# A hand-kept order table replaced by another one that also carries banks, fillers and load gates

## The chip, the cores and the metric

The kernel runs on one core of a Trainium2 chip. The core has five instruction queues that run side by side and wait for each other through semaphores: TensorE (PE, matmuls into the eight banks of PSUM), VectorE (DVE), ScalarE (ACT), GpSimd (POOL, used here to issue loads) and SyncE (SP, used here to issue transposes and stores). The metric is the device time of one execution in microseconds.

## The reference

Two stages follow each other. First comes attention for 4 batches, 8 heads, 768 positions and a head size of 64, in which a query sees the 8 first keys and the 96 nearest ones, with a bias that falls with distance. Then the result, laid out as 3072 tokens by 512, goes through a feed-forward layer with a squared ReLU. All arrays are float32 in memory. Cut to what matters:

```python
scores = scale * np.matmul(q, k.transpose(0, 1, 3, 2))
is_global = pos[None, :] < 8
is_local = (rel >= 0) & (rel < 96)
dist = np.where(is_global & ~is_local, 96, np.abs(rel))
scores = np.where(is_global | is_local, scores - slopes[:, None, None] * dist, -1e9)
a = softmax(scores)
x = np.matmul(a, v).transpose(0, 2, 1, 3).reshape(3072, 512)
h = np.maximum(x @ w_in, 0.0)          # w_in 512 x 2048
out = (h * h) @ w_out                  # w_out 2048 x 512
```

## The kernel before

The 3072 tokens are worked on as eight halves of 384 tokens, two for each batch (`hb` 0 to 7, with tiles of 128 tokens). Halves 0 and 1, the opening, run tile by tile in small jobs, since the data is still coming in; the others run in larger jobs. Everything is fp16 in SBUF, and sums are kept in PSUM in float32.

The stations of a half, with the lines that the profile shows, are these. `list_loads` (L472) lists the loads of q, k and v, three tiles of 128 tokens each, issued from POOL. Weights come the same way: `w_in_sb` in four column blocks c0 to c3 (`load_w_in`, L534) and `w_out_sb` in four row blocks (L541). In the opening q and k are turned (transposed to have the head's columns on partitions) on PE, `turn_first` and its neighbours (L1318, L1361); from half 3 on they are turned by a DMA transpose on SP, `turn_by_dma` (L647), one for k (`k<-sk`) and one for q (`q<-sq`). `score_unit` (L691, in the opening L1404) multiplies q by k into `sp`; its operands use 64 of the array's 128 rows, two heads at a time. ACT takes the exponent (`ex`, L704), DVE multiplies by the mask (`phat`, L728), PE multiplies by v (`av`, `attend`, L752), and DVE divides by the sum (`tm`, L762). `to_x_by_dma` (L777) turns the result by four DMA transposes on SP, `xt<-tm`, one for each pair of heads (the X transposes below); in the opening PE does it (`trx`, L1483).

Layer 1 (`hps`, L797, and L900 for halves in which it is done with seven products of mixed blocks in place of eight) multiplies by `w_in_sb`. The mixed blocks `x_mix` (L878) are made of xt on DVE. The ReLU and the square run on ACT and DVE (`hr`, `h`, `kept`). Layer 2 (`yps`, L1052, and L1138 for pairs of halves done by seven products) multiplies by `w_out_sb` or its mixed blocks `w_mix`; ACT or DVE copies or adds the result to `y` (L336, L338, L1200), and SP, once ACT, stores it (L1068, L1212, L1219, L1223). `L336` and `L338` are the two lines of `copy` for ACT and for DVE.

The order is not left to a scheduler. Each job of a station is an `Op` in one of three lists: PE's jobs (letter p), loads (l), and the rest. A table of words, `ORDER`, names for each step an engine (p, l, a for ACT, d for DVE, g for POOL, s for SP) and an index of the list; the ops are emitted in that order, so the table fixes each engine's queue, and for ops that could run on ACT or on DVE also the engine. While it walks the table, `Plan.run` keeps a small model of the time: it picks the PSUM banks that in the model come free first (`idle_banks`), and it gives a PE job in the first 24 us that in the model must wait a number of filler matmuls on zeros ahead of it (`warm`, L404 and L353), which keep PE busy. A load's order on the POOL queue comes from the table; what it must wait for comes from the code. There, the first k load (`sk`) of a half beyond the third waits for both turns of the half before, and the k turn of a half waits for the last of its q loads, and so for all of its q and k loads.

Of the kernel before, what the change touches and what calls it, by code (L numbers as in the profile page):

```python
# [41 lines left out]
AFTER = [0, 0, 0, 0, 0, 0, 0, 0]  # L42
# [10 lines left out]
ORDER = """d1 g2 a4 p0 a6 s8 d12 a0 s10 d17 l3 d13 l1 a18 a16 a19 l2 d21 d20 a27 l5 a26 d14 a22 d15 d3 a28 d5  # L53
p10 l4 a25 d9 p5 a30 d146 l0 a24 p1 a11 p2 d7 l6 a23 p3 l10 a32 d31 a33 d34 p6 l9 a29 d36 p7 a39 p11
d35 l7 p8 a46 p4 d43 p9 a41 l8 d37 p13 d44 a40 p12 d45 a47 l11 p14 d38 p16 a42 p15 d48 l13 p17 d51
a49 p19 p24 a52 l12 d55 p20 d64 p22 a50 p23 d58 l14 a53 p34 d56 p30 a60 p25 d71 p28 l16 p21 a81 d59
p26 d57 a82 l18 p27 d69 d67 p31 a65 d68 p18 a61 p29 l15 d72 p36 p32 a54 d70 p35 l19 a86 d66 p33 a73
d85 p39 d62 p40 l17 a74 a77 d76 p37 l21 d91 a78 p41 l20 d79 d63 p38 d83 l23 a101 d75 d84 p45 l22 a89
a87 d96 p44 l27 p47 a92 d80 p48 d107 a97 l29 d111 p46 a98 p52 l28 p43 a93 d110 p53 p42 d105 l30 d119
p55 d120 p50 l24 p59 a122 a88 d90 d99 a102 p51 l25 d106 a103 d94 p49 a116 a128 d108 p67 d100 a129  # L60
d95 a117 d112 p57 a104 p65 d125 p54 p58 d121 d189 p63 p61 p62 a132 d126 a109 p60 a114 d135 d118 a113
d115 p56 a127 d205 d191 a133 p74 a130 p72 a169 d138 p73 a165 d131 p77 d123 a166 p69 a167 p75 d156
d147 a157 p70 p71 d134 a158 p82 d159 l34 a162 d168 p81 a163 d186 l26 a170 p83 a142 p68 l31 d174 a139
d160 d149 p84 l35 a184 a164 d208 p64 a187 d124 l33 d161 a171 d148 a144 p85 l32 d272 a143 d206 p88
d207 l36 p89 d201 p79 d151 p86 a198 a178 d204 p91 d152 a195 a199 d188 p76 d202 a136 d150 p87 a172
d200 a179 p90 a196 d180 a193 p80 d153 a209 p78 s194 l37 p66 d155 a175 d203 a137 p95 d210 p92 a176
d223 a173 p94 d197 s224 l38 a185 d177 p100 a211 l39 d236 a181 s216 p93 a140 d237 p96 a182 p103 d238
s217 p97 d183 a244 a240 d221 a141 p102 d219 a222 d154 p106 s220 d213 d225 p98 p104 d239 s226 p99
d227 d228 p105 a234 d214 s229 d145 a218 d243 p101 l44 d245 d246 p107 l43 s215 d212 a241 d190 p109
l40 p110 p108 p111 a255 d192 l42 a251 p112 a256 d258 l45 a248 d257 p113 l41 a249 d230 d232 a252 p118  # L70
d259 p114 a273 d253 s260 l46 p116 d254 p115 a261 p120 d231 d250 l47 a262 p122 a264 p124 l48 s235
d280 p123 a265 d263 p131 a268 d233 a283 p127 d281 p126 a288 p132 d285 a269 p134 d295 s328 a287 p129
d270 a286 p119 a291 p142 d266 a293 p140 d296 s329 d314 p130 a311 p135 d267 a299 p128 d315 a292 p137
d274 a312 p136 d300 s242 p121 a305 s282 d327 a302 p125 a306 d289 p138 s275 a284 d303 p141 a307 d301
d304 a276 p117 d294 s290 a313 d308 p133 a271 l50 p139 d330 a278 p143 d297 a309 l56 p145 d279 a316
s298 p146 d310 p147 l53 a317 p144 d405 a334 l51 d322 p148 a326 a337 d323 l52 p149 a335 d443 d340
a331 l49 p151 d324 a341 p150 a332 d336 p152 l54 a342 d318 d325 p157 a348 p153 a343 d333 a345 d344
p159 p156 a346 d320 d319 a354 d407 p158 a356 p161 d321 a338 p172 d355 a359 p154 d349 p162 d377 a351
p169 p163 d360 a372 s378 l57 p164 d363 p167 a361 p166 d365 p171 d347 a368 p177 s408 a369 p160 d339
p165 a364 p170 a362 d357 p178 s409 l55 d373 a386 p175 a366 p173 a387 d382 p180 a367 p174 d376 p182  # L80
d374 p176 a379 s247 d383 p155 d380 s277 a384 s358 p179 d391 a385 p181 d395 a375 p168 s381 d353 d410
a393 p183 l58 a352 p184 d388 a370 a397 d394 l65 s396 p185 a392 d389 a399 d371 l62 p187 a398 d390
p188 p186 a419 l59 p189 d411 a415 a423 d412 l63 p190 a420 d426 a416 p191 d422 l73 a424 d414 a417
p192 l61 d421 a428 d425 p193 p194 p196 a432 l60 d413 a427 d418 a429 p198 p195 a436 d406 a444 d401
a433 p200 d492 p199 d402 a437 d447 p207 a430 p210 d435 a457 p204 s448 d445 p215 a462 p211 d453 p202
s350 d463 s446 p197 d439 a451 p203 d403 a464 p218 d496 d404 p206 a442 d441 d505 a475 d493 p205 a465
d438 p208 s507 p219 a455 d434 p213 a476 p201 d468 s508 a454 d431 a458 p223 p222 a472 d497 p214 a484
d469 d452 p217 a449 p212 s400 d470 a474 p209 d482 a456 p220 p227 d459 a477 s483 d466 p224 a500 p216
d495 a478 s467 l64 p221 d498 a471 p241 d479 a486 p225 l70 p229 a509 d488 d494 l66 p226 a489 d473
p228 a511 d490 a539 l69 d480 p231 d481 p233 l72 p230 a513 d501 d487 a519 l67 d460 p234 a520 d499  # L90
a512 l71 s440 p248 d521 a485 s506 d503 p235 l68 a514 d502 d522 a546 d510 p247 a461 d491 p236 s523
l74 d524 p237 a545 p232 d515 p239 a525 d531 a516 p246 d504 a517 p256 d544 p245 a536 p270 a528 d561
s537 d543 p240 a529 p249 d518 a538 p267 a547 d530 p251 a580 p255 d550 p252 a526 s595 p258 d559 a562
p243 a551 p266 d527 p238 a585 d578 s450 a553 p253 a565 d591 p254 s579 d541 a535 d554 p261 a557 p257
d532 s560 a568 p268 a558 d533 p242 a582 d555 s596 d563 a552 p260 d534 p250 a581 p269 d548 p264 p244
a567 a586 d574 p263 d542 a564 p259 d572 p262 a540 a583 p265 d556 p272 a575 s573 a597 d566 p271 d600
s549 d569 p277 d598 a576 d584 a599 p273 d570 a577 p274 d571 p275 p276 a601 d613 a608 d615 s614 l75
p278 a602 s593 d589 d616 a609 p279 a619 d617 s594 a604 p283 d587 a620 s592 d603 a611 a605 p281 d618
a631 p280 p282 a624 d588 p286 d606 a628 a625 p284 d634 a629 p287 d610 p292 a636 p288 d607 a632 d627
a635 d686 p294 a621 p301 d630 a646 p291 d637 d643 p299 d657 a641 p314 d626 a622 p290 d680 p285 d640  # L100
p307 s681 a633 p305 d623 p300 a665 p295 d655 s642 p293 s612 d647 d590 p296 d668 a644 p298 a656 d648
p309 a658 p289 d649 p308 a670 d654 p297 p304 d638 a651 p311 d652 s639 a663 p312 p306 d669 p317 d687
s653 p310 d688 a690 p302 d676 p316 p320 a684 s677 a650 p303 a685 d674 p328 p319 d671 a662 d666 a697
a672 p313 d659 p315 d696 p331 a675 d682 p318 a660 d691 d667 d678 a719 p333 a661 p332 d689 p321 d692
a664 d683 p335 d695 a716 p352 d698 d705 s699 p347 d693 s645 p334 d742 a752 p322 d723 a722 d673 p337
p339 d679 p336 d706 p338 d700 d720 p324 d721 d728 p329 a725 d753 a724 p343 a710 d729 p341 a726 d701
s711 p342 a717 p340 d736 p323 d694 a737 d734 p344 a738 d702 p345 d709 p325 d703 a740 d708 d707 p351
a712 d731 p353 a730 p326 d727 d704 p346 d750 p348 d713 a741 p327 d732 a733 p349 d714 p357 d746 a715
a754 d735 p330 d743 a755 d739 p354 d751 d764 p350 d744 a756 p356 d718 a748 s757 d747 a745 d749 p355
d760 p362 a758 d761 p358 d765 s759 d763 p368 a770 d779 a768 d767 p364 d762 d766 p359 d769 d775 p360  # L110
d776 d786 a783 p365 d790 d780 d781 p366 a787 d777 p367 a771 a788 p371 d789 d772 d782 s773 p361 d778
d794 p369 s795 d774 p370 d791 p363 d792 s793 p372 a784 p373 d796 s785 s797 a798 a799"""


class Op:
    EARLY = {"ACT": 0.035, "DVE": 0.045}
    LATE = {"ACT": 0.1, "DVE": 0.07}

    def __init__(self, costs, emit, needs, rank=0, lag=0.0, move=None):
        self.emit, self.rank, self.lag, self.move = emit, rank, lag, move  # L120
        self.needs = [n for n in needs if n is not None]
        self.costs = {e: c - self.EARLY.get(e, 0.0) for e, c in costs.items()}
        self.done, self.bufs = None, []
        self.wait = 0.0
        self.takes, self.users, self.rows, self.follows = 0, [], False, []


class Buffer:

    def __init__(self, tag, count):  # L130
        self.tag, self.count, self.users, self.taken = tag, count, [], False
# [7 lines left out]
class Plan:  # L139
# [5 lines left out]
    HOP = 0.08  # L145
    ENTER = 0.19
# [4 lines left out]
    def __init__(self, warm_from, warm_until):  # L151
        self.warm_from, self.warm_until = warm_from, warm_until
        self.queues = {"PE": [], "LOAD": []}
        self.rest = []
        self.free = {e: 0.75 for e in ("ACT", "DVE", "POOL", "SP")}
# [54 lines left out]
    def ready(self, op):  # L210
        t = self.free_at(op)
        if t is None:
            return None
# [1465 lines left out]
```

## Time and profile before

| | |
|---|---|
| median of 3 runs | 201.06 us (200.97 to 201.07) |
| span of the profiled execution | 200.3 us |
| PE busy | 193.0 us, 96% |
| DVE busy | 178.9 us, 89% |
| ACT busy | 155.9 us, 78% |
| POOL busy | 66.7 us, 33% |
| DMA | 27.52 MB |

The execution that the profiler recorded has no time of its own beside its span; the median of the runs lies 0.76 us above that span. Busy shares of the engines are of the span. A busy PE can still be waiting in part, since the ends of matmuls are modelled. In groups and waits, `<-` names what ended an idle time. "L" with a number is a line of the kernel before.

### The profile page before, as it was taken

The numbers are of one execution on the slowest core, as the hardware profiler recorded it, in microseconds if no ns is written. First come the engines' busy times: TensorE is split into PE (matmuls) and PEld (weight loads), VectorE is DVE, ScalarE is ACT, GpSimd is POOL, SyncE is SP. The second block draws the span as 40 slices with busy tenths as digits, with TensorE's granted clock in tenths as the row PEclk, the third lists the DMA queues.
The fourth block names the chain that finished last, engine by engine and source line by source line (L and its number), as shares of the span: only waits on it lengthen the run. The fifth ranks groups of instructions, "written<-read, shape, count | busy, mean of one in ns | idle before, by whom it ended". The sixth has DMA issues, their size and how long they took to land.

```text
span 200.3 us, 5912 instructions
## 1 busy us (share of the span) xinstructions
PE 193.0 (96%) x2346; PEld 161.3 (81%) x2346; DVE 178.9 (89%) x457; ACT 155.9 (78%) x335; POOL 66.7 (33%) x82
## 2 busy tenths in 40 slices
PE   7798999999999899999999999999999999999994
PEld 2685899766897587779878798899888988899993
DVE  7688698899999799989999999999989979998881
ACT  5999676898946889988999798989996669457411
POOL 8996564087108602920095019400000000000000
PEclk9999999999999999999999999999999999999999
DMA  5999999999999999999999989995230330210214
GB/s 154 180 150 197 187 181 173 209 192 154 176 203 74 141 206 219 120 115 99 221 133 147 155 203 144 166 246 111 53 114 3 124 61 3 105 56 0 108 52 157
DMA packets 106987, 27.52 MB, mean 137 GB/s; under 512 B 97104, under 2 KB 104016, under 8 KB 106960
## 3 DMA queue, kind: packets, MB, share of 16 engines
q0 software_dynamic: 74944, 13.11, 93.3%
q1 hardware_dynamic: 30816, 13.45, 30.9%
q10 hardware_dynamic: 1200, 0.59, 1.1%
q8 instruction: 18, 0.29, 0.6%
q14 instruction: 9, 0.07, 0.1%
HBM read 27.26 MB, written 6.29 MB: 167 GB/s over the span
## 4 chain that ended last, share of the span: by engine, by line
PE 72%; DVE 12%; DMA 7%; POOL 3%; ACT 2%; issue 1%; DVEq 0%; POOLq 0%
PE yps L1138 28%; PE hps L797 17%; PE hps L900 17%; DMA w_in_sb<-in_moe_w_in_dram 4%; PE sp L691 3%; PE av L752 3%; DMA xt<-tm 3%; PE yps L1052 2%; DVE phat L728 2%; POOL w_mix L472 2%; DVE tm L762 2%; POOL v L472 1%; ACT ex L704 1%; DVE hr L958 1%; DVE mixed L1103 1%
## 5 line engine op out<-in xcount | busy, mean ns | idle before, releaser
L797 PE MATMUL hps<-xt,w_in_sb 128*128 128x384 f16 (+2 forms) x336 | 45.1, 280 | 0.2 <-DMA w_in_sb<-in_moe_w_in_dram 0.2
L704 ACT ACTIVATE ex<-sp 128x512 f16<-128x512 f32 x66 | 36.4, 632 | 2.6 <-PE sp L691 2.5
L1138 PEld LDWEIGHTS <-h 128*128 128x128 f16 x376 | 34.3, 98 | 5.1 <-DVE h L838 0.2
L797 PEld LDWEIGHTS <-w_in_sb 128*128 128x128 f16 x336 | 28.1, 98 | 7.9 <-DMA w_in_sb<-in_moe_w_in_dram 0.7
L336 ACT COPY y<-yps 128x256 f32<-128x256 f32 (+2 forms) x42 | 15.5, 389 | 17.5 <-PE yps L1138 17.3
L1138 PEld LDWEIGHTS <-mixed 128*128 128x128 f16 x272 | 25.1, 98 | 3.7 <-DVE mixed L1103 0.6
L958 DVE TENSOR_TENSOR hr<-hps,kept 128x384 f16<-128x384 f32 x49 | 25.6, 551 | 2.2 <-ACT h L998 1.1
L472 POOL DMA_DIRECT2D sq<-in_q_dram x19 | 17.2, 907 | 29.7 <-DMA q<-sq 21.6
L336 ACT COPY kept<-hps 128x384 f32<-128x384 f32 x45 | 21.1, 490 | 7.4 <-PE hps L900 4.9
L822 ACT ACTIVATE hr<-hps 128x384 f16<-128x384 f32 (+1 forms) x44 | 22.2, 530 | 4.9 <-PE hps L797 4.8
L472 POOL DMA_DIRECT2D sk<-in_k_dram x19 | 17.1, 901 | 25.3 <-DMA q<-sq 13.6
L900 PEld LDWEIGHTS <-in_mix 128*128 128x128 f16 x272 | 23.0, 98 | 2.3 <-DVE x_mix L878 0.6
L900 PE MATMUL hps<-x_mix,in_mix 128*128 128x192 f16 x204 | 23.4, 246 | 0.3 <-ACT ex L704 0.3
L1138 PE MATMUL yps<-w_out_sb,h 128*128 128x256 f16 (+1 forms) x184 | 22.5, 268 | 0.1
L1138 PE MATMUL yps<-w_mix,mixed 128*128 128x256 f16 (+1 forms) x184 | 22.4, 268 | 0.1
L1138 PE MATMUL yps<-w_mix,h 128*128 128x256 f16 (+1 forms) x192 | 22.4, 264 | 0.0
L472 POOL DMA_DIRECT2D v<-in_v_dram x24 | 21.5, 908 | 2.6 <-DMA w_mix<-in_q_dram 0.9
L728 DVE TENSOR_TENSOR phat<-ex,mask 128x1024 f16<-128x1024 f16 (+1 forms) x36 | 20.7, 598 | 0.0
L900 PEld LDWEIGHTS <-w_in_sb 128*128 128x128 f16 x204 | 17.4, 98 | 2.1 <-issue 0.7
L900 PE MATMUL hps<-xt,w_in_sb 128*128 128x192 f16 x136 | 16.1, 246 | 0.5 <-DMA xt<-tm 0.5
L998 ACT ACTIVATE h<-hr 128x768 f16<-128x768 f16 x19 | 15.9, 853 | 0.4 <-DVE hr L968 0.3
L836 ACT ACTIVATE h<-hr 128x512 f16<-128x512 f16 (+1 forms) x22 | 15.9, 742 | 0.1
(115 smaller groups left out, 363.4 us busy)
## 6 DMA issues: line engine op xcount, KB each, us to landing
out_dram<-y SPq DMA_DIRECT2D x23, 256.0 KB, 2.5
v<-in_v_dram POOLq DMA_DIRECT2D x24, 128.0 KB, 6.8
sq<-in_q_dram POOLq DMA_DIRECT2D x19, 128.0 KB, 6.7
sk<-in_k_dram POOLq DMA_DIRECT2D x19, 128.0 KB, 6.7
w_in_sb<-in_moe_w_in_dram POOLq DMA_DIRECT2D x4, 512.0 KB, 10.9
w_out_sb<-in_moe_w_out_dram POOLq DMA_DIRECT2D x4, 512.0 KB, 12.3
y<-in_q_dram SPq DMA_DIRECT2D x2, 256.0 KB, 4.4
y<-in_k_dram ACTq DMA_DIRECT2D x2, 256.0 KB, 5.1
```

The source lines that it names most:

```text
L336: nc.scalar.copy(out=out, in_=in_)
L472: dma = nc.gpsimd.dma_start(out=dst, in_=src[x.b, :, r0 + t * P:r0 + (t + 1) * P, :] .rearrange("h p d -> p h d"))
L691: nc.tensor.matmul(sp[h][:, i, :], lhsT=lhsT, rhs=x.q[rows, r % HT, a, :], start=True, stop=True)
L704: nc.scalar.activation(out=st["ex"][:, h], in_=sp[h], func=AF.Exp, scale=scale)
L728: eng(e).tensor_tensor(out=x.phat[a][:, :, t0:t0 + n], op=ALU.mult, in0=st["ex"][:, :, i0:i0 + 2 * n].rearrange("p e (t b) c -> p e t (b c ...
L797: nc.tensor.matmul(st["ps"][:, i * n:(i + 1) * n], lhsT=w_in_sb[:, kk, m * P:(m + 1) * P], rhs=x.xt[:, kk, c0:c1], start=kk == 0, stop=kk ...
L822: nc.scalar.activation(out=o, in_=i, func=AF.Relu)
L836: nc.scalar.activation(out=h2, in_=hr, func=AF.Square)
L900: nc.tensor.matmul(st[name][:, i * HC:(i + 1) * HC], lhsT=left(i, kk), rhs=right(kk), start=fresh and i == kk == 0, stop=kk == KK - 1, ski ...
L958: eng(e).tensor_tensor(out=hidden(which)[:, :, cols], in0=sums(name), in1=st[kept], op=ALU.add)
L998: nc.scalar.activation(out=h2, in_=hr, func=AF.Square)
L1138: nc.tensor.matmul(st[bank_name][:, 0:n], lhsT=a(m), rhs=b(m)[:, cols], start=fresh and m == 0, stop=m == HK - 1, skip_group_check=not fresh)
```

## The change

The operations stay the same; what stands where changes, in four ways.

1. `ORDER` is another table, with another order on each of the queues and for some ops another engine. Its words carry more. `p100.5` gives the PSUM bank of a job (`.57` two banks, 5 and 7), `+149` the filler time ahead of it in hundredths of a microsecond, and `l43@220` a gate: the load is issued only once the SP transfer 220 of the list has landed.
2. The model of the time in `Plan` (`ready`, `free_at`, `take`, `idle_banks`, `by_rank`) goes. `run` reads the table.
3. The waits of transfers in the code change. From half 4 on, a k load waits for the k turn of the half before and a q load for the q turn, where the first k load waited for both. A k turn waits for k's loads and a q turn for q's, where the k turn waited for all.
4. PE's turns of the opening also stand behind the memset of v's last column (`x.bt.op`, L485 in its `start`).

The instruction lists as built: PE 2366 matmuls for 2346, which are fillers (26 transposes of 128 columns, all ahead of the first tile's turn, for six wide matmuls); DVE 476 instructions for 459 and ACT 323 for 340; POOL and SP as many as before. The runs of 64-row score matmuls between other work are 23 for 17.

```diff
@@ (the table; one stretch of each, around 55 us, and the end)
-... d202 a136 d150 p87 a172
-d200 a179 p90 a196 d180 a193 p80 d153 a209 p78 s194 l37 p66 d155 a175 d203 a137 p95 d210 p92 a176
-...
-p370 d791 p363 d792 s793 p372 a784 p373 d796 s785 s797 a798 a799"""
+... p104 s220 d221 p106 d213 a222 d228 a218 p99 d227 s229 d154 p107 d239 a234 d212 p110.04
+s226 l43@220 p109.37 d245 p101 a255 d246 a251 l41 p111 a256 d241 s215 a252 l42@224 p116.06 s235
+d258 p114.32 s242 d257 p108.47 l40@229 p112 a248 d230 d253 d192 p120 a249 a261 d254 p118.4 a262
+p115.73 l44@226 d273 p113 a264 d231 d263 l45 p122.2 a265 d250 p124 a268 p125.7 l46 d267 a269 d280
+...
+p372 d790 p373 d796 p371 s797 a798 a799 p363 d794 s795 a784 s785"""
@@ class Plan
     def run(self):
-        order = []
-        self.in_rows = False
-        for e, op in self.by_table() if ORDER else self.by_rank():
-            start = max(self.ready(op), self.free.get(e, 0.0))
...
-            taken = self.idle_banks(op.takes) if op.takes else []
...
-            if taken and start < self.warm_until:
-                self.spare = start - 0.1 - max(idle, taken[-1][0])
-                self.spare *= 0.5 if start < self.warm_from + 5.0 else 1.0
...
+        lists = {"p": self.queues["PE"], "l": self.queues["LOAD"]}
         for word in ORDER.split():
+            word, _, spare = word.partition("+")
+            word, _, banks = word.partition(".")
+            word, _, gate = word.partition("@")
+            op = lists.get(word[0], self.rest)[int(word[1:])]
+            self.now, self.spare = [int(i) for i in banks], int(spare or 0) / 100
+            op.result = op.emit("POOL" if word[0] == "l" else self.LETTERS[word[0]])
+            if gate:
+                self.behind(op.result, self.rest[int(gate)].result)
@@ list_loads
-        before = (prev.turned if prev else []) + (halves[x.hb - 1].turned if x.hb > 2 else [])
+        if x.hb > 3:
+            before = {"sk": halves[x.hb - 1].turned[:1], "sq": halves[x.hb - 1].turned[1:]}
+        else:
+            last = halves[x.hb - 1].turned if x.hb > 2 else prev.turned if prev else []
+            before = {"sk": last, "sq": last}
...
-                if x.hb > 3 and name == "sk" and t == 0:
-                    for turn in halves[x.hb - 1].turns + (prev.xturns if AFTER[x.hb] else []):
-                        behind(dma, turn)
-                if name == "sq":
-                    x.last_load = dma
+                return dma
@@ turn_by_dma
-                if not x.turns:
-                    behind(turn, x.last_load)
                 x.turns.append(turn)
+                return turn
-            op = plan.add({"SP": 2.0 if i else 1.5}, emit, [*x.k_in, *x.q_in, x.bt.op, *late],
+            op = plan.add({"SP": 2.0 if i else 1.5}, emit, [*loads, x.bt.op, *late],
                           move=plan.TURN)
```

More of the change, by code (lines that the diff above doesn't have):

```diff
@@ L130, in __init__ @@
     def __init__(self, tag, count):
[L131 removed]
+        self.tag, self.count, self.users = tag, count, []
     def used_by(self, *ops):
@@ L189, in load @@
         return op
-    def free_at(self, op):
-        t = self.last_move if op.move else 0.0
-        for buf in op.bufs:
-            ring = self.rings.setdefault(buf.tag, [])
-            if buf.taken or ring:
-                t = max(t, buf.start if buf.taken else ring[-1].start)
-            if not buf.taken and len(ring) >= buf.count:
-                for u in ring[-buf.count].users:
-                    if u.done is None:
-                        return None
-                    t = max(t, u.done + self.HOP)
-        return t
@@ L247, in by_table, with run @@
[L247 removed]
+    def run(self):
         lists = {"p": self.queues["PE"], "l": self.queues["LOAD"]}
         for word in ORDER.split():
[L250 to L281 removed]
@@ L1642 @@
     with tc.manual_schedule():
-        order = plan.run()
+        plan.run()
 _INS = ['q', 'k', 'v', 'n_global', 'n_local', 'moe_w_in', 'moe_w_out']
```

212 lines of the change are left out of this document (73 added, 139 removed).

## The prediction

> **What bounds the kernel now.** I read the page's busy times and slices first, then the waits of TensorE (PE), its windows, the chain that ended last, and last the queues around its two weak stretches.
>
> ```profile
> span 200.3 us, 5912 instructions
> ...
> PE 193.0 (96%) x2346; PEld 161.3 (81%) x2346; DVE 178.9 (89%) x457; ACT 155.9 (78%) x335; POOL 66.7 (33%) x82
> ...
> PE   7798999999999899999999999999999999999994
> ...
> PEclk9999999999999999999999999999999999999999
> ```
>
> TensorE is busy 96% of the span at full clock; DVE stands second with 89%. So the time is PE's own work plus the few microseconds in which PE has nothing to do. The profiled span of 200.3 us lies 0.76 us under the median run of 201.06; I carry that 0.76 to the forecast.
>
> ```profile
> 20.00:30.00 10.00, 9.95 (x138) 8.98 (x139) 8.32 (x29) 6.80 (x15) 6.12 (x8) 1.00 1.76 184
> 30.00:60.00 30.00, 30.00 (x349) 24.02 (x348) 27.14 (x63) 23.54 (x53) 11.73 (x14) 1.00 1.80 184
> 60.00:70.00 10.00, 9.42 (x103) 6.30 (x102) 8.69 (x22) 7.07 (x15) 7.92 (x9) 1.00 1.70 108
> 70.00:80.00 10.00, 10.00 (x127) 8.19 (x125) 9.63 (x27) 9.26 (x22) 1.30 (x2) 1.00 1.82 211
> 80.00:90.00 10.00, 9.53 (x115) 7.47 (x112) 9.18 (x23) 9.20 (x20) 6.58 (x8) 1.00 2.29 119
> 90.00:100.00 10.00, 10.00 (x132) 8.83 (x130) 9.86 (x27) 9.05 (x19) 0.00 (x0) 1.00 1.33 156
> 100.00:110.00 10.00, 9.97 (x143) 8.36 (x141) 9.71 (x23) 9.98 (x24) 7.88 (x9) 1.00 1.97 145
> 140.00:185.00 45.00, 45.00 (x509) 40.04 (x507) 41.50 (x101) 32.80 (x69) 0.00 (x0) 1.00 0.20 59
> ```
>
> These windows list PE, weight loads, DVE, ACT and POOL. After 20 us PE idles 0.58 us in 60 to 70 and 0.47 us in 80 to 90, and next to nothing elsewhere. Before 20 us it waits for data, which ends with the first columns of w_in:
>
> ```profile
> 11.57 8.42 DMA w_in_sb<-in_moe_w_in_dram
> 20.04 3.69 PE hps L797 x40
> ...
> 45.31 0.78 PE sp L691 x24
> 46.09 0.97 PE yps L1052 x4
> 47.06 0.87 PE yps L1138 x8
> ...
> 48.58 0.86 PE yps L1052 x4
> ...
> 50.32 0.55 PE sp L691 x16
> ...
> 61.78 5.83 DMA xt<-tm
> ...
> 81.85 1.06 PE yps L1138 x8
> ...
> 83.85 1.05 PE yps L1138 x8
> ```
>
> In the chain (start, duration, work) the weights issued at 11.57 let layer 1 start at 20.0. Two later groups of eight `yps L1138` matmuls take 1.06 and 1.05 us where a full-speed one takes 0.87: 0.37 us more of PE's waiting that the windows count as busy. With 0.58 and 0.47 this makes 1.42 us lost between 60 and 90. The chain there goes back to one transfer, the DMA transpose that turns attention's result into layer 1's input (`xt<-tm`, L777), 5.83 us long.
>
> ```profile
> 58.06 4.92 SPq L777 DMA_TRANSPOSE xt<-tm  x3
> ```
>
> ```profile
> 60.67 1.75 POOL L472 DMA_DIRECT2D sq<-in_q_dram  x2 [9.90 <-DMA q<-sq]
> 62.41 1.82 POOL L472 DMA_DIRECT2D sk<-in_k_dram  x2
> ```
>
> ```profile
> 67.70 0.63 DVE L878 TENSOR_TENSOR x_mix<-xt 128x384 f16<-128x384 f16 x2 [1.17 <-DMA xt<-tm]
> ```
>
> ```profile
> PE hps L900 <- DMA xt<-tm: 0.5, 1, 0.5
> ```
>
> ```profile
> DMA to landing us min/median/max: 2.3/3.8/7.5
> ```
>
> SP issues three of these transposes from 58.06 on; POOL starts the next half's loads at 60.67, the moment the q turn has landed, beside them. DVE then waits 1.17 us for the last transpose and PE 0.5. Over all 24 transposes the time to landing runs from 2.3 to 7.5 us, so 5.83 is a crowded one.
>
> **The change part by part.** It keeps every matmul of the result and moves three things: the order on each queue, the waits of the loads and turns, and the engine of some copies.
>
> *Start.* After adds 26 idle-time transposes of 128 columns before the first tile and drops six wide fillers; the cover is the wait for the first tile. POOL's list now starts tokens without a wait: before, it lost 0.31 us to DVE's memset of v (L485), which after puts first on DVE.
>
> ```profile
> 5.41 1.84 POOL L472 DMA_DIRECT2D v<-in_v_dram  x2 [0.31 <-DVE v L485]
> ...
> 11.57 1.55 POOL L534 DMA_DIRECT2D w_in_sb<-in_moe_w_in_dram  x2
> ```
>
> The w_in load stands at the same place of POOL's list, so it issues 0.31 earlier, and layer 1 may start as much earlier: bounds 0 (if the DMA engines and not the issue set its landing) and 0.31. I take 0.30, because POOL issues back to back from there. If PE's opening work became the cover that fails, the term goes to 0.
>
> *Score runs.* Attention's scores use 64 rows of the array; each run of such matmuls costs entry and exit. From the chain: 24 matmuls take 0.78 and 16 take 0.55, so one is 0.029 and entry is 0.55 - 16 x 0.029 = 0.09; the four `yps L1052` behind a run take 0.97 against 0.86 elsewhere, so exit is 0.11. A run costs 0.20. The built order has 23 runs where before has 17. Four more stand in the opening, where PE waits for data anyway; one group of eight scores is moved behind the first layer-1 job, which costs 8 x 0.029 + 0.20 = 0.43, and two more runs stand later: 0.40. Sum +0.83, bounds 0.56 (only exit counted) and 0.95 (0.24 a run).
>
> The Trainium skill, page "TensorEngine Tiling (Array Packing)", section Key Properties, speaks against this part too: a change of tiling mode drains the array. Its page "TensorE: Matmul & The Clock Gate", section Step-by-step, gives a drain of about 128 cycles, an estimate of 0.05 us for each change at 2.4 GHz, 0.11 for a run in place of the 0.20 measured here; by it this term would be 0.56 and the forecast 200.3.
>
> *Transposes and loads.* A load word in the new table may carry a gate: it is issued only when a named SP transfer has landed. Half 4's q and k loads are gated behind half 2's X transposes (those of 58 us), and some loads of the later halves behind one transpose or another. In return k's turn waits for k's loads alone, not for the last load of all. The X transposes of 58 us thus run with no loads beside them. In the quiet case they take 2.3 instead of 5.83, 3.5 us, which is more than the 1.42 us lost, so I take all of 1.42; bounds 0 (the loads only move, and something else crowds them) and 1.42. Behind a gated load the whole POOL list waits, v's loads too; k and q of half 4 then land some 1 to 2 us later. Their turn is late only if that eats its lead. In before SP issues half 4's turns at 71.93 and 73.55:
>
> ```profile
> 71.93 1.45 SPq L647 DMA_TRANSPOSE k<-sk  x1
> 73.55 2.95 SPq L647 DMA_TRANSPOSE q<-sq  x1
> ```
>
> ```profile
> DMA to landing us min/median/max: 3.7/4.3/6.2
> ```
>
> This second row of landings is that of the turns (L647): the one issued at 73.55 lands near 78. Counted back from PE's end, the scores that need it stand at about 80 us in the new order, a lead of some 2 us for the 1 to 2 us of delay. The quiet transposes also open the gates sooner; so I take nothing, with a bound of +1.7.
>
> *Engines.* The built order gives DVE 476 instructions for 459 and ACT 323 for 340: 17 copies and squares go from ACT to DVE. Costs from these groups:
>
> ```profile
> L336 ACT COPY y<-yps 128x256 f32<-128x256 f32 (+2 forms) x42 | 15.5, 389 | 17.5 <-PE yps L1138 17.3
> ```
>
> ```profile
> L1200 DVE TENSOR_TENSOR y<-yps,y 128x256 f32<-128x256 f32 x28 | 11.7, 422 | 1.6 <-ACT ex L704 0.7 <-PE yps L1138 0.4 <-issue 0.2
> ```
>
> An op of that kind is 0.39 on ACT and 0.42 on DVE, 17 x 0.40 = 6.8 us more for DVE, from 178.9 to about 185.7, 93% of the span. Beside PE's 96% this is still cover, so it costs nothing in the sum. If the cover is gone, see the second rival.
>
> *End.* Before ends with a half-width copy and small store; after ends with an older job whose 256 columns go out whole.
>
> ```profile
> 196.50 0.37 ACT L336 COPY y<-yps 128x256 f32<-128x256 f32 x1 [3.54 <-PE yps L1138]
> ...
> 197.39 0.27 ACT L336 COPY y<-yps 128x128 f32<-128x128 f32 x1 [0.52 <-PE yps L1138]
> 197.69 0.36 ACTq L1219 DMA_DIRECT2D out_dram<-y  x1
> ```
>
> ```profile
> out_dram<-y SPq DMA_DIRECT2D x5, 256.0 KB, 2.0
> ...
> out_dram<-y ACTq DMA_DIRECT2D x1, 64.0 KB, 1.7
> ```
>
> The copy takes 0.37 for 0.27 and the store lands in 2.0 for 1.7: +0.40, with bounds 0.3 and 0.6.
>
> *Sum.* 200.3 - 0.30 + 0.83 - 1.42 + 0.40 = 199.81 us of span, plus 0.76: 200.57, called 200.6, 0.23% under 201.06. A measurement of this kernel can tell about 0.2%, that is 0.40 us, from no change: under 200.66 is faster, over 201.46 slower. The forecast lies just on the fast side.
>
> **The rivals.**
>
> *Half of it comes (no change).* The X transposes are quicker but DVE's own queue holds their users: in the rows above DVE is busy 9.63 of 10 us in 70 to 80, so an x_mix op that is released 1 us earlier may find its place in the list no earlier. Then of 1.42 half stays: 200.57 + 0.71 = 201.3. With nothing gained at all, the same sum gives 202.0. For it: DVE waited for the transposes only 1.17 us in this row, and later losses at 82 and 84 us stand behind DVE and ACT work. Against it: those losses begin with that wait.
>
> *DVE becomes the bound (slower).* DVE's idle time in 70 to 110 is 0.37 + 0.82 + 0.14 + 0.29 = 1.62 us. A proportional share of the 6.8 us moved to it, 40 of 200 us, is 1.4 us. Then DVE has no slack there; each wait that it still has for PE or ACT goes through to PE, whose banks it empties. If the 1.62 us of waits stay, PE loses up to that: 200.57 + 1.6 = 202.2. It decides from the point where more than about 0.9 us of them goes through (200.57 + 0.9 is past 201.46). For it: 9.86 busy of 10 in 90 to 100. Against it: ACT gives work away and was 9.98 busy of 10 in 100 to 110, so some of DVE's waits for ACT go, and in 140 to 185 DVE has 3.5 us to spare.
>
> *The gates hold the loads too long (slower).* A transpose with the longest landing, 7.5 for the 3.8 of the median, holds the gate 3.7 us longer; with a lead of 2 us, 1.7 us reaches the scores: 200.57 + 1.7 = 202.3. For it: everything on POOL stands behind one gate. Against it: a gated transpose is a quiet one, nearer 2.3.
>
> **How the numbers follow.** The forecast case, in which all 1.42 us or nearly all of it comes, has 0.41. No change has 0.26: half of the gain, or all of it eaten by a run price of 0.24. DVE as the bound has 0.19, late gates 0.14. So faster 0.41, same 0.26, slower 0.33. The point stays that of the likeliest, 200.6, whose own range is 199.8 to 200.66. The low end is 200.57 with the run price by exit alone (0.56 for 0.83, so 200.3), the tail at its lower bound (-0.1) and the remaining idle time of 20 to 30 and 100 to 110 (0.08) gone, and 0.3 more for waits hidden in busy time as at 82 us: 199.8. The high end, 202.3, is that of the late gates, and takes in DVE as the bound.
>
> **What would show it.** Right: PE idle under 0.2 us in 60 to 90, no row in which x_mix or hps waits for xt; first hps of layer 1 at about 19.7; transposes to landing with a maximum near 4; the last store of 256 KB on SP. The run price is right if `yps` or `hps` groups behind score runs stay near 0.1 us longer. DVE as bound would show as PE waiting for DVE (x_mix, kept, hr) and DVE over 9.8 of 10 in 70 to 110. Late gates would show as POOL waiting for `xt<-tm` and PE's `sp L691` waiting for the k or q turn. The prediction is wrong in its first step if layer 1 starts no earlier, and as a whole if PE's idle time in 60 to 110 is not smaller than before.

## The result, and the profile after

The changed kernel takes 209.3 us (median of four runs, 207.8 to 211.9) against 201.06 before: 1.036 times the time of before, with an interval of 1.028 to 1.045. The forecast was 200.6, with a range of 199.8 to 202.3. Times of one and the same kernel spread by some per cent between executions, the kernel before included (199.9 to 206.0 over all its comparison runs), so ratios with their intervals are used below, and single profiles to see where time goes. An execution more than 1.5% longer than the shortest of its kernel is left out of the ratios, and the profiles of three kernels ("v loads ungated, no fillers", "old order, new waits" and "before, memset first") are of such long executions, so what they alone show is not taken for a cause.

One base number of the forecast falls at once. Each comparison run lists its time beside its span, and the two lie 1.7 to 1.9 us apart (208.78 and 207.0 for the profile below). The 0.76 that the prediction carried compared the span of one execution with the median of others; the profiled execution of before took about 202.1 (an estimate from that distance). In spans the comparison is 200.3 before, 199.8 forecast, 207.0 after: 7.2 us off.

The page of the changed kernel, span, busy times and slices:

```profile
span 207.0 us, 5957 instructions
...
PE 197.3 (95%) x2366; PEld 164.5 (79%) x2366; DVE 183.5 (89%) x474; ACT 149.6 (72%) x318; POOL 66.9 (32%) x82
...
PE   7999999999999999499999999998999999999993
...
PEclk9999999999999999759999999999999999999999
```

One slice of PE stands out, and right behind it the granted clock falls. The waits of PE, and windows around that place (PE, weight loads, DVE, ACT, POOL, then the clock):

```profile
PE yps L1057 <- DVE h L757: 2.9, 1, 2.9
...
PE av L670 <- DMA vb<-v: 0.7, 1, 0.7
```

```profile
60.00:70.00 10.00, 10.00 (x115) 7.27 (x113) 8.91 (x22) 7.75 (x15) 7.01 (x8) 1.00 0.99 127
70.00:80.00 10.00, 10.00 (x129) 8.20 (x128) 9.84 (x29) 7.63 (x17) 1.57 (x3) 1.00 1.70 172
...
82.00:86.50 4.50, 1.61 (x20) 1.14 (x20) 1.35 (x5) 3.49 (x8) 0.08 (x1) 0.89 1.75 153
86.50:92.30 5.80, 5.80 (x39) 3.97 (x40) 5.08 (x11) 1.74 (x5) 5.18 (x6) 0.50 1.35 89
```

From 60 to 82 us PE is never idle, where before lost 0.58 in 60 to 70. Then it stands still for 2.89 us, and after that works for 5.8 us at half clock, which costs another 2.9 in this execution. The chain that ended last says why:

```profile
59.35 2.90 DMA xt<-tm
...
63.78 1.72 POOL sk L395 x2
65.49 6.77 DMA sk<-in_k_dram
...
72.40 5.49 DMA k<-sk
...
78.44 6.82 DMA v<-in_v_dram
...
85.28 0.31 DVE vb L257
...
85.90 0.48 DVE h L757
...
86.42 4.88 PE yps L1057 x22
```

Four transfers follow each other, with 3.2 us of issuing on POOL between the first two and next to nothing between the others: an X transpose of half 2 opens the gate of half 4's first q load (`l43@220`), behind which the k loads stand in POOL's list; the last k load lets half 4's k turn go; the k turn opens the gate of half 4's third v load (`l48@328`); and that load lands at 85.26. Queues of POOL and DVE at that place:

```profile
62.90 0.88 POOL L395 DMA_DIRECT2D sq<-in_q_dram  x1 [10.69 <-DMA xt<-tm]
...
78.44 0.96 POOL L395 DMA_DIRECT2D v<-in_v_dram  x1 [8.43 <-DMA k<-sk]
...
86.42 1.77 POOL L395 DMA_DIRECT2D sk<-in_k_dram  x2 [6.14 <-DMA xt<-tm]
```

```profile
85.28 0.62 DVE L257 COPY vb<-v 128x520 f16<-128x520 f16 x2 [3.01 <-DMA v<-in_v_dram]
85.83 0.54 DVE L757 TENSOR_TENSOR h<-hr 128x768 f16<-128x768 f16 x1
```

POOL issues its list in order, so each gate also holds what stands behind it: the k loads at 63.78 come right behind the q load that waited 10.69 us. DVE waits 3.01 us for the v load with its copy into `vb`, and the square `h` that PE needs for layer 2 stands behind that copy. It needs no v at all.

On the half clock: the Trainium skill, page "TensorE: Matmul & The Clock Gate", section "Part 1: The HAM clock gate", says that the array's clock drops to half after an idle window of about 3.4 us and that the window runs free. The trace agrees on the half (0.50 granted). On the length it differs: 0.89 granted over the 4.5 us from 82 means that the last 1.0 of them ran at half, so the clock fell near 85.5, 2.0 us after PE's last matmul had ended at 83.53, and it stayed down until about 92.3. The measurement decides.

How much this adds differs between executions. The four runs of the changed kernel list a mean granted clock of 0.984 (the profiled one), 0.989, 0.992 and 0.997 over their spans, which makes, as an estimate, 6.6, 4.6, 3.4 and 1.2 us at half clock. The one with the least of it still took 207.8 us. So the 2.9 us are the price in the profiled execution, and the slowdown does not hang on them alone.

The start and the end of the kernel, first the opening matmuls on zeros, the fillers and the first layer-1 matmuls, then the last matmuls, copies and stores (start, duration, engine, line, operation):

```profile
1.39 3.59 PE L323 MATMUL warm<-early 128*128 128x512 f16 x8 [1.39 <-DVE early L1457]
4.78 2.68 PE L275 MATMUL trp<-ident,early 128*128 128x128 f16 x26
...
20.73 1.49 PE L716 MATMUL hps<-xt,w_in_sb 128*128 128x128 f16 x20
```

```profile
202.54 1.04 PE L1057 MATMUL yps<-w_mix,h 128*128 128x256 f16 x8
202.74 0.42 DVE L1119 TENSOR_TENSOR y<-yps,y 128x256 f32<-128x256 f32 x1 [1.03 <-PE yps L1057]
203.19 1.15 SPq L1142 DMA_DIRECT2D out_dram<-y  x2
203.62 0.37 ACT L255 COPY y<-yps 128x256 f32<-128x256 f32 x1 [1.48 <-PE yps L1057]
```

Layer 1 starts at 20.73 (20.04 before), and from the last matmul's modelled end, 203.58, to the end of the span pass 3.42 us (2.95 before, 197.35 to 200.3).

### The profile page after: what moved, and what is told of

Read it like the earlier page. It is cut to its first block, busy times and chain, and to the rows that moved or that the text cites. A ratio compares the mean times of both kernels' runs of the same rounds, so it can differ in the third digit from the quotient of the medians.

```text
span 207.0 us, 5957 instructions
## 1 busy us (share of the span) xinstructions
PE 197.3 (95%) x2366; PEld 164.5 (79%) x2366; DVE 183.5 (89%) x474; ACT 149.6 (72%) x318; POOL 66.9 (32%) x82
## 2 busy tenths in 40 slices
DMA packets 106987, 27.52 MB, mean 133 GB/s; under 512 B 97104, under 2 KB 104016, under 8 KB 106960
## 4 chain that ended last, share of the span: by engine, by line
PE 66%; DMA 15%; DVE 10%; ACT 4%; issue 2%; POOL 1%; POOLq 0%; DVEq 0%; SPq 0%; ACTq 0%
PE yps L1057 22%; PE hps L716 16%; PE hps L819 13%; DMA v<-in_v_dram 3%; DMA sk<-in_k_dram 3%; PE av L670 3%; DMA vb<-v 3%; DMA k<-sk 3%; PE sp L609 3%; PE yps L971 2%; DMA out_dram<-y 2%; PE warm L323 2%; DMA xt<-tm 1%; DVE mixed L1022 1%; PE trp L275 1%
## 5 line engine op out<-in xcount | busy, mean ns | idle before, releaser
L716 PE MATMUL hps<-xt,w_in_sb 128*128 128x384 f16 (+2 forms) x336 | 45.6, 280 | 0.0
L622 ACT ACTIVATE ex<-sp 128x512 f16<-128x512 f32 x66 | 35.6, 627 | 4.6 <-PE sp L609 4.4
L1057 PEld LDWEIGHTS <-mixed 128*128 128x128 f16 x272 | 25.8, 101 | 4.1 <-issue 0.3
L255 ACT COPY kept<-hps 128x384 f32<-128x384 f32 x42 | 20.0, 492 | 9.2 <-PE hps L819 8.4
L1057 PE MATMUL yps<-w_out_sb,h 128*128 128x256 f16 (+1 forms) x184 | 23.2, 273 | 2.9 <-DVE h L757 2.9
L255 ACT COPY y<-yps 128x256 f32<-128x256 f32 (+2 forms) x36 | 13.6, 396 | 15.9 <-PE yps L1057 13.3
L741 ACT ACTIVATE hr<-hps 128x384 f16<-128x384 f32 (+1 forms) x40 | 20.0, 532 | 6.2 <-PE hps L716 6.0
L1057 PE MATMUL yps<-w_mix,mixed 128*128 128x256 f16 (+1 forms) x184 | 24.1, 281 | 0.0
L755 ACT ACTIVATE h<-hr 128x512 f16<-128x512 f16 (+1 forms) x23 | 16.6, 738 | 2.7 <-PE yps L1057 2.0
L917 ACT ACTIVATE h<-hr 128x768 f16<-128x768 f16 x16 | 13.5, 851 | 2.5 <-DVE hr L887 2.5
```

The source lines that it names most:

```text
L255: nc.scalar.copy(out=out, in_=in_)
L622: nc.scalar.activation(out=st["ex"][:, h], in_=sp[h], func=AF.Exp, scale=scale)
L716: nc.tensor.matmul(st["ps"][:, i * n:(i + 1) * n], lhsT=w_in_sb[:, kk, m * P:(m + 1) * P], rhs=x.xt[:, kk, c0:c1], start=kk == 0, stop=kk ...
L741: nc.scalar.activation(out=o, in_=i, func=AF.Relu)
L755: nc.scalar.activation(out=h2, in_=hr, func=AF.Square)
L917: nc.scalar.activation(out=h2, in_=hr, func=AF.Square)
```

## The experiments

Theory A: a chain of gates makes one v load late, DVE is blocked behind it, PE behind DVE, and the idle time halves the clock. Theory B: the new order as such is slower, through DVE's 17 more operations or otherwise. All ratios are to the kernel before, measured beside it on the same chip.

| kernel | ratio, interval | span of its profile |
|---|---|---|
| changed | 1.036 (1.028 to 1.045) | 207.0 |
| one gate off | 1.021 (1.014 to 1.027) | 202.2 |
| no gates | 1.015 (1.010 to 1.020) | 203.0 |
| no gates, once more | 1.015 (1.010 to 1.020) | 204.3 |
| stall filled | 1.013 (1.005 to 1.021) | 204.0 |
| copy moved back | 1.013 (1.005 to 1.020) | 204.0 |
| no fillers | 1.029 (1.020 to 1.039) | 207.5 |
| v loads ungated, no fillers | 1.017 (1.007 to 1.027) | 207.1 |
| old order, new waits | 1.006 (1.000 to 1.012) | 204.7 |
| old order, one v gate | 1.011 (1.006 to 1.015) | 200.5 |
| old order, quiet X | 1.019 (1.014 to 1.024) | 205.1 |
| no gates, nine ops to ACT | 1.021 (1.016 to 1.027) | 205.4 |
| no gates, old tail | 1.017 (1.011 to 1.023) | 203.3 |
| no gates, old waits | 1.013 (1.009 to 1.016) | 203.2 |
| before, memset first | 1.001 (0.997 to 1.005) | 201.5 |

**One gate off.**

```diff
-... s282 d327 l48@328 p136 p134.6
+... s282 d327 l48 p136 p134.6
```

> The changed kernel with one gate taken off: the third v load of half 4 no longer waits for half 4's k turn (l48 in place of l48@328). Theory A, one chain of gates (X transposes, then k loads, then k turn, then this v load) blocks DVE for 3.0 us and PE for 2.9, and PE then runs 5.8 us at a granted clock of 0.50: the stall at 82 to 86 us goes, the clock is 1.00 throughout, and the span falls by 2.9 + 2.9 = 5.8 us from 207.0 to about 201.2, the time from about 209 to 203. Theory B, the new order is slower as a whole because DVE carries 17 more operations: the stall goes but other waits take its place, and the span stays over 204.

The stall and the drop of the clock are gone: PE is busy 10.00 of 10 in each window from 60 to 100, and the span is 202.2, 1.0 above A's 201.2. PE's wait for `vb<-v`, 0.7 us in the changed kernel, is 1.4 here, at 130 to 140. Theory A holds for the place; but the ratio is still 1.021, so this gate is not all of it, and B is not out.

**All gates off.** Each `@...` of the table is dropped.

> The changed kernel with all 16 gates off; waits for buffers stay. Theory A: as with one gate off or a little faster, since two later v loads are freed too (PE's wait of 0.7 us for vb near 136 to 147), unless the loads now crowd the X transposes of 58 us again, which would give back up to 1.4 us: span 200.5 to 202.5. Theory B: span over 204. A theory C, that the gates protect the X transposes as they were meant to: landing of the X transposes of 58 us from under 4 us back to over 5, and PE idle in 60 to 80.

With 203.0 and a ratio of 1.015 the gates cost some 2% of the 3.6. The span lies between what theories A and B allow. At 58 us theory C fails: the X transposes there land in 4.4 us at most and PE idles 0.08 us in 60 to 80. One of half 3, at 81.4, takes 7.73 us: PE is busy 8.96 in 80 to 90 and waits 0.6 us for `xt<-tm`, 0.6 for `x_mix`, where with one gate off it is busy 10.00. The second profile without gates shows the same (7.93 us, 8.80 of 10). So by these profiles the other gates did keep those transposes clear; the gates together cost more than that saved.

**Stall filled.** The wait stays; PE is kept busy through it.

```diff
-p148.0 d322 ...
+p148.0+290 d322 ...
...
                     st[bank_name] = bank([P, 512], FP32, "yps")
+                    for _ in range(int(plan.spare / 0.216)):
+                        nc.tensor.matmul(st[bank_name], lhsT=w_in_sb[:, 0, 0:P],
+                                         rhs=w_in_sb[:, 0, 0:512], start=True, stop=True)
```

> The changed kernel, gate in place, with 13 filler matmuls of 512 columns (2.8 us) ahead of the layer-2 job in which PE stalls. Theory A: the load lands as late as before and DVE waits as long, but PE stays busy, so its clock stays at 1.00; the 2.9 us lost to the half clock come back less the two or three matmuls that the fillers push behind the wait (0.2 to 0.5 us): span about 204.5, time about 206.3. If the clock's drop has another cause than PE's idle time, the clock still falls and the span stays at 207.

Its windows and the fillers among PE's rows:

```profile
80.00:84.00 4.00, 3.77 (x47) 2.39 (x45) 3.23 (x9) 3.66 (x8) 1.32 (x2) 1.00 1.20 147
84.00:88.00 4.00, 4.00 (x27) 2.35 (x25) 2.81 (x7) 2.40 (x6) 0.51 (x1) 1.00 1.54 140
88.00:92.00 4.00, 4.00 (x59) 3.46 (x57) 3.73 (x10) 3.12 (x8) 4.00 (x6) 1.00 1.20 76
```

```profile
84.06 2.97 PE L1056 MATMUL yps<-w_in_sb 128*128 128x512 f16 x13
```

The clock stays at 1.00 and the span falls by 3.0 to 204.0, though 13 matmuls were added. So the clock's drop came of the idle time, and between these two profiles it is worth about as much as the idle time itself.

**Copy moved back.** The load stays late; only its consumer on DVE moves.

```diff
-... p146.57 d405 a313 p144.4 ... d340 a341 l52 d318 a338
+... p146.57 a313 p144.4 ... d340 a341 l52 d318 d405 a338
```

> The changed kernel, gate in place, with the DVE copy that waits for the late v load (d405, v to vb of half 4) moved behind six other DVE operations in DVE's queue. Theory A: the load is as late, but the square that PE waits for no longer stands behind it: the stall goes or shrinks to under 0.5 us, clock 1.00, span about 201.2 to 202. If instead PE's stall came from the v load itself (matmuls that read v), nothing changes: 207.

PE's wait for `h` is gone and no clock under 1.00 shows at 80 to 100, with the gate in place. What stalled PE was the place of a waiting copy in DVE's queue, not the data. At 88.7 PE waits 0.9 us for `phat` in its place, more than the 0.5 expected, and the span reached 204.0 only, since other late transfers now show: PE waits 1.4 for half 6's q turn, at 123.3, and 1.6 for `vb<-v`.

**No fillers.**

```diff
-d9 ... p1.12+149
+d9 ... p1.12
```

> The changed kernel without its 26 filler transposes ahead of the first tile's turn. In its trace they run from 4.99 to 7.47 us, 0.095 us each, and the first turn starts right behind them, where before it started at 6.18; layer 1 starts at 20.73 where before it started at 20.04. Theory A (the fillers outlast the wait that they were to fill): the first turn starts at about 6.3, layer 1 at 19.8 to 20.1, and the span falls by 0.6 to 0.9. Theory B (layer 1 waits for something else in the opening, ACT's exponents or the loads): layer 1 still starts after 20.5 and the span stays within 0.3. The stall at 83 to 86 us stays in both.

Layer 1 starts at 20.07 here, as theory A has it, but the second half of A fails: the span is 207.5, not 0.6 to 0.9 under 207.0, and the ratio of 1.029 (1.020 to 1.039) overlaps that of the changed kernel. The stall for `h` is still there with 2.3 us, and PE waits 1.7 for a q turn and 1.3 for `vb<-v` besides. And the next kernel, also without fillers, started it at 20.88, after a clock of 0.52 and 0.50 between 8 and 10 us; with fillers other runs show 20.12 to 20.73. The fillers took 2.68 us in the changed kernel and 1.61 in the one without gates, 0.103 and 0.062 each. The turns of the opening wait for the fillers in one case and run at the lower clock in the other; which is better is not settled by these runs.

**v loads ungated, no fillers.** The gates of `l48`, `l55`, `l57`, `l65`, `l73` go, and `l64` moves ahead of `l65`; q and k loads keep theirs.

> The changed kernel with the gates of the five v loads off, half 6's first v load moved ahead of the gated loads before it, and no fillers; the gates of the q and k loads stay. Theory A (v loads held behind the k turns and behind gated loads are the loss): no PE wait over 0.5 us after 25 us, clock 1.00, span 199 to 200.5, so the time is level with before or a little faster. If the span stays over 202, the loss lies in the order of DVE, ACT and PE and not in the loads.

The expectation fell. By the ratio the time is 1.7% over before, not level. The chain of the profiled execution, which took 208.9 us (the two that make the ratio took 205.1 and 206.0), leads to the next user of a gated load:

```profile
113.24 7.00 DMA sq<-in_q_dram
120.26 5.80 DMA q<-sq
```

PE waits 3.8 us in all for q turns (three times, 2.4 the longest), and the clock falls to 0.87 at 120 to 130. The q turn is that of half 6, for which PE also waits 1.4 us in the kernel with the copy moved back. So a late q turn costs there too; how much of it is in the two shorter executions is not shown.

**Old order, new waits.** The table of before, with the banks and fillers that its model gave, run by the changed code.

> The order of before, with the banks and fillers that its model chose, run by the changed code: only the waits of turns and loads differ (a k turn waits for k's loads alone, a k load for the k turn alone). Theory A: within 0.5% of before, since a wait of 0 to 1 us less for the k turn feeds nothing that PE waits for. A theory D, that the new waits themselves let transfers collide and cost time: over 1% slower.

A ratio of 1.006, from 1.000 to 1.012: by it the new waits alone are no gain, and at most a small loss. But the ten executions run from 201.3 to 206.5 us, and the profile is of the longest. Its q turn at 56.66 takes 5.55 us, and half 4's loads start behind it, 2.1 us later than before (62.78 for 60.67):

```profile
62.78 1.84 POOL L393 DMA_DIRECT2D sq<-in_q_dram  x2 [12.07 <-DMA q<-sq]
```

```profile
60.00:70.00 10.00, 10.00 (x122) 7.21 (x120) 9.17 (x24) 7.82 (x16) 7.21 (x9) 1.00 1.27 102
...
80.00:90.00 10.00, 8.17 (x98) 6.38 (x98) 8.41 (x19) 8.26 (x18) 7.61 (x9) 1.00 1.88 139
90.00:100.00 10.00, 8.04 (x115) 7.32 (x114) 8.16 (x23) 6.40 (x15) 0.00 (x0) 1.00 1.20 98
```

PE loses nothing in 60 to 70 here, and 1.83 and 1.96 us in 80 to 100, to `xt<-tm` and `x_mix`. There is no gate in this kernel.

**Old order, one v gate.** As the last, with `l48@328` put behind `s328`.

> As e7, with a single edit: the third v load of half 4 is gated behind half 4's k turn, as in the changed kernel. In the old order DVE copies that v at 77.1 us; the k turn issued near 72 lands near 78, the v load then takes 6.8 to land, near 85. Theory A: DVE is blocked for 7 to 8 us, PE for 5 to 7, and its clock is halved for some 6 us after: span up by 8 to 10 us over e7. Theory B: the old order has slack for it, under 2 us.

I was wrong by far: 1.011 against 1.006, intervals overlapping, and a profile of 200.5 in which PE has no wait for it. I had taken another copy for this load's; its own stands at 81.84 us. The load, issued at 77.25, landed in 4.6 us, where the changed kernel's took 6.82 from 78.44, and DVE shows no wait there. The same gate costs 4.8 us of span in the one order (207.0 against 202.2) and no stall in the other.

**Old order, quiet X.** The forecast's central term by itself, in the old order with the new waits.

```diff
-... l44 ...
+... l44@226 ...
```

> The old order and its banks in the changed code, with one gate: the first load of half 4 waits until the third of the four X transposes at 58 us has landed. This is the part that the forecast took 1.42 us for. If the forecast's term was right: the last X transpose lands in under 4 us in place of 5.8, DVE and PE no longer wait for it, and the time falls by 1 us or more against before. If the loads' delay of 2 to 4 us costs as much further down the chain (k turn, q turn, scores near 84 us): level or slower.

The chain, the POOL and SP queues and windows of this kernel:

```profile
59.75 3.25 DMA xt<-tm
...
84.44 7.16 DMA xt<-tm
```

```profile
63.66 1.75 POOL L393 DMA_DIRECT2D sq<-in_q_dram  x2 [13.08 <-DMA xt<-tm]
```

```profile
74.62 1.45 SPq L564 DMA_TRANSPOSE k<-sk  x1
76.25 2.63 SPq L564 DMA_TRANSPOSE q<-sq  x1
...
79.62 6.04 SPq L693 DMA_TRANSPOSE xt<-tm  x4
```

```profile
60.00:70.00 10.00, 10.00 (x121) 7.20 (x120) 9.17 (x24) 7.71 (x16) 6.34 (x8) 1.00 0.98 91
70.00:80.00 10.00, 10.00 (x118) 7.77 (x114) 9.04 (x26) 9.51 (x22) 2.00 (x3) 1.00 1.67 193
80.00:90.00 10.00, 7.76 (x96) 6.15 (x96) 8.21 (x19) 8.01 (x18) 7.41 (x9) 1.00 2.00 142
90.00:100.00 10.00, 8.58 (x118) 7.48 (x117) 8.16 (x23) 6.78 (x15) 0.00 (x0) 1.00 1.07 95
```

The transpose of 58 us takes 3.25 for 5.83, and the 0.58 us lost in 60 to 70 are back. The k turn starts 2.7 us later than before (74.62 for 71.93), and the next half's transposes meet the next loads: one of them takes 7.16. PE then loses 2.24 and 1.42 us in 80 to 100. The expected gain did not come: 1.019. The rival "the loads' delay costs further down" fits, but this trace does not show that the gate is what does it, since the same order without the gate ("old order, new waits") takes the same course: k turn at 74.39, 3.8 us lost in 80 to 100. What the two share is that half 4's loads start late, at 62.78 and 63.66; where they start at 60.67 (before) and 60.97 (one v gate), PE loses 0.47 and 0.92 us in 80 to 100. In the last experiment below they start at 62.54, and it loses 2.65. The gate seems to make the late start the rule: its six executions take 205.4 to 208.7 us, the ten without it 201.3 to 206.5 on another chip. That the late start causes the waits is argued from these five profiles.

**Nine operations to ACT.** In the new order without gates, `d273 d284 d291 d292 d306 d317 d385 d392 d398` become `a...`.

> The new order with no gates and nine operations between 60 and 130 us (three holds and three squares among them) given back from DVE to ACT, at the same places of the order, so some 4 us of work leave DVE. If DVE is what binds the new order without gates: 1 to 1.5% faster than the new order without gates. If DVE waits for transfers and PE rather than binding, or ACT's longer squares (0.85 against 0.48 us) now come late: the same or slower.

1.021 against 1.015 for the order without gates: no gain, rather a loss. DVE's extra work is not what binds.

**Old tail.** In the new order without gates, the group `p363 d794 s795 a784 s785` moves ahead of `p372`. The hand-out `d794` then stands ahead of its bank's last product, so that part of the last tile lacks one product; the instructions are the same in number and kind.

> The new order with no gates, its last layer-2 job and its two stores put back ahead of the final chain, as before had it, so that a half-width copy and a 64 KB store end the kernel. Expected from the rows: from the last matmul's end to the span's end 3.0 in place of 3.4 us, so 0.4 to 0.5 us (0.2%) under the new order without gates; if the job that is moved up then waits for its operands, less.

From the last matmul's end to the span's end it is 2.9 us (200.40 to 203.3), 3.37 in the order without gates (200.93 to 204.3). The term is there; in the ratio, 1.017 against 1.015, it is not seen.

**No gates once more**, for the comparison.

> The new order with no gates once more, as the comparison for the two runs above: 1.0 to 2.0% slower than before, as it was in its first run (1.5%).

As in its first run.

**No gates, old waits.**

> The new order without gates and with the waits of before (a k turn behind the last q load, the next half's first k load behind both turns). If the new waits cost by letting loads run into the X transposes: 0.5% faster than the new order without gates, so about 1.0% over before. If the order itself is the cost: unchanged, 1.3 to 1.6% over before.

1.013 (1.009 to 1.016): some 0.2% under the same order with new waits, inside the intervals. So the order itself is what stays, not the waits.

**Before, memset first.** In the old table `d3` moves up to stand right behind `d1`; the changed code runs it, with the waits of before put back.

> The kernel before with one edit: DVE sets v's last column first of all, so POOL's third token load no longer waits 0.31 us for it. If the start term was right: w_in's first block issues at 11.26 for 11.57, layer 1 starts near 19.73 for 20.04, and the time falls by 0.3 us (0.15%). If the landing is set by the DMA engines or PE's opening work is the bound: layer 1 starts at 20.0 as before.

w_in's load issues at 11.40 for 11.57, and layer 1 starts at 20.00 for 20.04. The trace shows 0.04 us of the start term's 0.30. The ratio of 1.001 (0.997 to 1.005) is too wide to tell 0.15%. This profile loses nothing in 60 to 70 and 2.24 us in 80 to 90, where PE waits for `xt<-tm`: the old table takes the late course with the old waits, too.

## Why the prediction was wrong

*What bounds the kernel.* PE at full clock, with its idle time as the only thing to win: right as far as it goes. What I passed over is the row of the DMA engines on the page of before:

```profile
DMA  5999999999999999999999989995230330210214
```

They are busy nine tenths or nearly that until some 135 us. In the changed kernel the same row is:

```profile
DMA  5999999999978999996998999999370140040133
```

It falls to 7 and 8 at 57 to 67 us, where POOL waits for the first gate until 62.9, and to 6 at 93 to 98, and its nines last to some 145 us, for the same 27.52 MB. I read only the transposes' landings, as if the loads that were moved out of their way cost nothing. That the idle time of the DMA engines is itself a loss is argued from the two rows and not tested. A nine is also no proof of a full engine: in the slices with nines before moves between 74 and 246 GB/s.

*Transposes and loads (forecast -1.42, taken whole).* This step failed, and it is most of the miss: the gates were priced at a gain of 1.42 us with a bound of +1.7, and in the profiled execution one of them brought a stall of 2.89 us and 2.9 us of half clock. Without that gate the span is 4.8 us shorter; without any, the ratio falls from 1.036 to 1.015.

The gain was mis-sized before the gates came in. Of its 1.42 us, 0.19 were never there. The piece of 1.06 us ends at the modelled end of its last matmul, because the chain goes on to ACT there:

```profile
81.85 1.06 PE yps L1138 x8
...
83.21 0.61 ACT ex L704
```

On PE itself sixteen of these matmuls take 1.92 us from 81.85, so the first eight take 0.87, which is full speed. The piece of 1.05 us has score matmuls behind it, which start 0.98 us after it does, and PE shows no wait there, so its 0.18 may be the entry into a score run; that is not settled. And the 0.58 us in 60 to 70 belong to the one execution that was profiled: the old table shows 10.00 of 10 there in other profiles without any gate on those loads, and loses more in 80 to 100 instead.

Of the step itself the first half came true: no wait for an X transpose and no idle time of PE from 60 to 82 (without gates it is 0.08 us). But the prediction named for half 4 only gates on q and k loads, and one of its v loads carries a gate too: the third stands behind half 4's own k turn. I priced one delay of 1 to 2 us against one lead of 2. In the trace four landings stand in series, 2.90, 6.77, 5.49 and 6.82 us. The rival "the gates hold the loads too long" was right in kind; its price (1.7) took one late transpose, and no transpose was late. The step also left out what stands behind the late load's user in DVE's queue, and the clock: 2.89 us of waiting cost another 2.9.

*Start (forecast -0.30).* It came as +0.69. The memset's wait was real, and its removal in the old order moves the load's issue by 0.17; layer 1 does not follow, which is the prediction's own sign that its first step is wrong. I had named PE's opening work as the cover that may fail, and in the changed kernel it did: the fillers end at 7.46, where before turned its first tile at 6.18, and without fillers layer 1 starts at 20.07 in one profile, though at 20.88 in the other.

*Score runs (+0.83).* Right, as far as rows show it, which is for 0.43 of it; the 0.40 for two more runs was not measured. The chain of the changed kernel, at the group that was moved behind layer 1's start:

```profile
24.67 0.33 PE sp L1323 x8
25.00 0.98 PE hps L716 x8
...
26.57 0.87 PE hps L716 x8
```

The group costs 0.33 + 0.11 = 0.44; forecast 0.43. The estimate from the drain that the Trainium skill gives (page "TensorE: Matmul & The Clock Gate", section "Step-by-step: what each phase is for"), 0.11 for a run, stays half of what is measured, and the measurement decides.

*Engines (0).* Right: DVE is busy 9.84 of 10 in 70 to 80 and PE has no idle time; giving nine operations back gained nothing. The rival of DVE as the bound has nothing for it here. DVE did matter, as a queue in which one waiting copy holds everything behind it.

*End (+0.40).* Measured 0.47.

The misses add up: 0.99 at the start, 2.89 of waiting, 2.9 of half clock, 0.7 for `vb<-v` and 0.07 at the end are 7.6 against the 7.2 between forecast and measured span; with what was not there to gain (0.19, or 0.37), up to 7.9. The 0.4 to 0.7 over is not resolved. Without gates the order stays 1.3 to 1.5% slower. Of the 2.7 us in its profile, 0.83 are score runs (as forecast, half of it measured), 0.47 the end and 0.10 the start; the rest, 1.3, is waiting, put down in its rows to late `xt<-tm`, `x_mix`, `mixed` and `h`. Which of the order's placements makes these late was not tried one by one, so the cause of this part stays open.

## What to carry to other kernels

When a change orders transfers behind one another, write down the whole chain of landings with its durations and follow each to the engine queue where its first user stands; a wait is priced by what stands behind the user, not by the user. Look at the busy share of the DMA engines before counting a delayed load as free. Before counting an idle time of half a microsecond as something to win, see whether it stands at the same place in a second profile of the same kernel. And where PE may stand still for some 3 us, look at the granted clock behind it: here the drop cost about as much again as the wait.

## What was not expected

A waiting time of 2.89 us was enough to halve PE's clock for the 5.8 us of work behind it, and 13 idle matmuls in that gap won 3.0 us of span. The same gate on the same load cost 4.8 us of span in one order, and in another it left no stall (1.011 against 1.006, with overlapping intervals). And in the opening the granted clock of the rows reads 1.00 while eight 512-column matmuls take 3.59 us, 0.45 each, against 0.23 (2.97 for 13) later, in the kernel with the filled stall: that column does not show PE's slow first microseconds.
